# Masks of one head pair moved from TensorE to GpSimd, with task priorities and lags from a timing model, in a windowed-attention and MLP-mixer kernel

## The chip, the cores and the metric

The kernel runs on one core of one Trainium2 chip. Times are device microseconds (us) of one execution. A core has five engines that work in parallel, each taking its own instructions strictly in order: TensorE (PE in the profile; PEld are its weight loads), VectorE (DVE), ScalarE (ACT), GpSimd (POOL), and SyncE (SP), which here issues transfers (DMA). An instruction waits until the data it needs have been announced by a semaphore, and everything behind it in the same engine's queue waits too (in the first timeline below ScalarE stands 2.83 us in front of one instruction). SBUF is the memory of the core in which the engines find their operands; PSUM banks (`ps_ga`, `ps_sb` and so on) are the buffers into which TensorE writes its results, and in this program another engine empties a bank before TensorE uses it again.

## The reference, cut to what matters

Four batches, 8 heads, 768 positions, head size 64. Each position sees the 4 first positions (the sinks) and the last 128. The attention result `x` goes through a token mixer and a channel mixer.

```python
scores = scale * np.matmul(q, k.transpose(0, 1, 3, 2))
keep = is_sink | ((rel >= 0) & (rel < window))        # window = 128, 4 sinks
a = softmax(np.where(keep, scores, -1e9))
x = np.matmul(a, v)                                   # then (B, S, H*D)
u = x + (relu(x.T @ w_tok1) @ w_tok2).T               # token mixer
out = u + relu(u @ w_ch1) @ w_ch2                     # channel mixer
```

## The kernel before

Work is cut into *groups* of 4 heads, two groups per batch, eight in all; a group has two *head pairs*, `j` = 0 and 1. So pair (1,0) is the first pair of the second group of the first batch. The program is a list of tasks, each with dependencies, a priority and an assumed duration. Before anything is emitted, `Plan.order` plays them through a timing model of the engines, and the order found there is the order in which each engine gets its instructions. Nothing is reordered on the chip.

The parts that matter, with cuts marked `# ...`:

```python
PE_MASKS = {0, 1}                      # groups whose masks TensorE adds
DMA_LAG, LATE_LAG, LATE_AT = 1.0, 4.0, 85
BIAS = {}                              # priority offsets by task
LATE_CAST = [None, None, ("POOL", "ACT", "DVE"), ("POOL", "ACT", "DVE"), ("POOL", "ACT", "DVE")]
MASK_ENG = {g: ("POOL",) if g > 3 else ("POOL", "DVE") for g in range(8)}
# ... in the model: when the model believes that a load has landed
finish(x.pop(0)[0], drained + (LATE_LAG if drained > LATE_AT else DMA_LAG if drained > 14 else 1.0))
# ... scores of one unit; with a TensorE mask, -30000 is put into the bank first
if first:
    for i in range(2):
        nc.tensor.matmul(bank(slot)[:, i, 0:w], ident, mneg[...], start=True, stop=False)
for kt, w in kts_of(u)[0]:
    for i in range(2):
        nc.tensor.matmul(bank(slot)[:, i, at:at + w], kT[...], qT[...], start=not first, ...)
# ... exp by ScalarE into pT; without a TensorE mask, pT is then multiplied or
#     selected to zero outside the window, by GpSimd or VectorE (m0, m1)
# ... group 4's loads of q and k are held back until the load of v of group 3 has landed
nc.sync.dma_start(out=scratch_b[0:1, 1:2], in_=va[(g - 1) % 2][...])
# ... each load of q or k (float32) is cast to bfloat16 by one engine out of LATE_CAST[g]
copy(t, dst[s][:, ts(j, NT)], src[s][:, 2 * j:2 * j + 2])
```

The softmax here doesn't subtract the row's maximum and nothing guards it: scores larger than these inputs give would overflow.

Of the kernel before, what the change touches and what calls it, by code (L numbers as in the profile page):

```python
# [14 lines left out]

LOADS = "v0 v1 tok1 tok2 ch1a ch1b ch1c ch2a ch2b q2 k2 v2 q3 k3 v3".split()
CAST_LOADS = set()
PE_MASKS = {0, 1}
DMA_TURNS = {5, 6, 7}
NO_GATE = True  # L20
EARLY, EARLY_PRIO = 4, 1.7
GATE_AT = (1, 1)
GATED = True
FIRST_CASTS = [["ACT", "DVE"], [("POOL", "DVE")] * 2, [("POOL", "DVE")] * 2, [("POOL", "DVE")] * 2]
V_PARTS = 1
DMA_CAST_PARTS = 2
DMA_LAG, LATE_LAG, LATE_AT = 1.0, 4.0, 85
BIAS = {}
ACT_MORE = 0.0
LATE_CAST = [None, None, ("POOL", "ACT", "DVE"), ("POOL", "ACT", "DVE"), ("POOL", "ACT", "DVE")]  # L30
MASK_ENG = {g: ("POOL",) if g > 3 else ("POOL", "DVE") for g in range(8)}

SEM = 0.05
PE_TAIL = 0.16


class Task:


    def __init__(self, eng, hold, fn, deps=(), prio=50, lat=None, need=None, slot=None, frees=False, dma=None, port=False):  # L40
        self.eng = (eng,) if isinstance(eng, str) else tuple(eng)
        self.hold, self.fn, self.prio = hold, fn, prio
        self.lat, self.need, self.slot, self.frees, self.dma = lat, need, slot, frees, dma
        self.port = port
        self.deps = [d for d in deps if d is not None]
        self.start = self.done = None
        self.left, self.users = 0, []

# [8 lines left out]
class Plan:  # L57
# [16 lines left out]
    def order(self, filler=None):  # L74
        for n, t in enumerate(self.tasks):
            t.n = n
            t.left = len(t.deps)
            for d in t.deps:
                d.users.append(t)
# [132 lines left out]
def pe(*cols):  # L212
    return sum(c / 2400 + 0.0025 for c in cols)
# [10 lines left out]
def pool(n, per=0.00086, base=0.12):  # L224
    return n * per + base
# [7 lines left out]
def kernel(  # L233
# [140 lines left out]
    def rows_in_turn(src, g, lo, hi):  # L374
        return heads(src, g, lo, hi).rearrange("h (p t) d -> p h (t d)", t=NT)
# [17 lines left out]
    def pair32(tile_, s, lo, hi):  # L393
        return tile_[s][:, lo:hi].rearrange("p h t d -> p h (t d)")
# [2 lines left out]

    def load_pair(g, which, j, eng, deps=(), prio=5):
        src, dst = ((q, q32), (k, k32))[which]
        return load(eng, pair32(dst, Gs[g].s, 2 * j, 2 * j + 2), rows_in_turn(src, g, 2 * j, 2 * j + 2), 1.12, deps, prio)  # L400

    for g in range(GB):
        for j in range(2):
            if g in CAST_LOADS:
                continue
            Gs[g].lq[j] = load_pair(g, 0, j, "SP", prio=next(order_prio))
            Gs[g].lk[j] = load_pair(g, 1, j, "ACT", prio=0)

    def load_v(g, deps=(), prio=5):
        n = GH // V_PARTS  # L410
# [11 lines left out]
    c1, c2 = DCH // N1, NF // N2  # L422
    L = {}
    for n, what in enumerate(LOADS):
        prio = EARLY_PRIO + 0.001 * n if n < EARLY else 3 + n
        gate = [gate_task] if n >= EARLY and GATED else []
        kind, g = what[:-1], what[-1]
        if kind == "v":
            L[what] = load_v(int(g), gate, prio=prio)
        elif kind in ("q", "k"):  # L430
            g = int(g)
            src, big, small = (q, q32, qb) if kind == "q" else (k, k32, kb)
            if g in CAST_LOADS:
                dst = small[g % 2].rearrange("p a i d -> p (a i d)").rearrange("p (h x) -> p h x", h=GH)
            else:
                dst = pair32(big, g % 2, 0, GH)
            L[what] = load("POOL", dst, rows_in_turn(src, g, 0, GH), 2.6 if g in CAST_LOADS else 2.1, gate if g else [], prio=prio)
        elif what == "tok1":
            L[what] = load("POOL", w_tok1, moe_w_tok1.rearrange("(t p) n -> p t n", p=P), 2.8, gate, prio=prio)
        elif what == "tok2":  # L440
            L[what] = load("POOL", w_tok2, moe_w_tok2.rearrange("(t p) n -> p t n", p=P), 2.2, gate, prio=prio)
        elif kind == "ch1":
            i = ts("abc".index(g), c1)
            L[what] = load("POOL", w_ch1[:, :, i], moe_w_ch1.rearrange("(t p) n -> p t n", p=P)[:, :, i], 2.85, gate, prio=prio)
        elif kind == "ch2":
            i = ts("ab".index(g), c2)
            L[what] = load("POOL", w_ch2[:, i], moe_w_ch2.rearrange("(t p) n -> p t n", p=P)[:, i], 4.3, gate, prio=prio)
# [50 lines left out]
    def pr(g, what, j=0):  # L498
        like = KIND.get(what, what)
        extra = BIAS.get(f"{what}{g}", 0) + (BIAS.get(f"{what}{g}.{j}", 0) if j else 0)  # L500
        if what == "ex" and g not in PE_MASKS:
            extra += 20
        if g < GB:
            return FIRST[like] + 0.5 * g + extra
        return (g // GB) * 10 + CH[like] + 0.5 * (g % GB) + extra
# [46 lines left out]
    def make_cast(g, w, j):  # L552
        G, s = Gs[g], g % 2
        old = Gs[g - 2] if g >= 2 else None
        src, dst, ld = ((q32, qb, G.lq), (k32, kb, G.lk))[w]
        free = [t for t in old.T[w]] if old else []
        if G.dma:
            n = GH // DMA_CAST_PARTS
            G.cast[w] = []
            for j in range(DMA_CAST_PARTS):  # L560
                def f(t, j=j):
                    copy(t, dst[s].rearrange("p a i d -> p (a i d)").rearrange("p (t h d) -> p h t d", t=NT, h=GH)[:, n * j:n * j + n],
                         src[s][:, n * j:n * j + n])
                G.cast[w].append(add("POOL", pool(384 * n), f, [*ld[n * j:n * j + n], *free], prio=pr(g, "ca")))
        elif g in CAST_LOADS:
            G.cast[w] = list(ld)
        else:
            def f(t):
                copy(t, dst[s][:, ts(j, NT)].rearrange("p t i d -> p i t d"), src[s][:, 2 * j:2 * j + 2])
            if g < GB:  # L570
                eng, hold = FIRST_CASTS[2 * g + j][w], {"POOL": pool(768), "DVE": 0.42, "ACT": act(768, True)}
            elif not G.dma:
                eng, hold = LATE_CAST[g], {"POOL": pool(768), "ACT": act(768, True), "DVE": 0.42}
            else:
                eng, hold = ("POOL",), pool(768)
            t = G.cast[w][j] = add(eng, hold, f, [ld[j], *free], prio=pr(g, "ca", j), port=True)
            if (g, j) == GATE_AT and w:
                gate_task.deps.append(t)

    def make_cv(g):  # L580
        G, s = Gs[g], g % 2

        G.cv = list(G.lv)
        if g < 2:
            G.cv.append(add("POOL", 0.12, lambda t: nc.gpsimd.memset(va[s][:, :, :, D:D1], 1.0), prio=1))

    def qkT(T, g, j):
        x = T[g % 2]
# [4 lines left out]
    def make_turn(g, w):  # L593
# [9 lines left out]
            G.T[w] = [t, t]  # L603
            return
        for j in range(2):
            slot = Slot()

            def f(t, j=j, slot=slot):
                ps = flat(slot).bitcast(BF16)
                for n in range(NT):  # L610
                    if g in CAST_LOADS:
                        x = (qb, kb)[w][s].rearrange("p a i d -> p (a i d)").rearrange("p (h t d) -> p h t d", h=GH, d=D)
                        for i in range(2):
                            nc.tensor.transpose(ps[ds(64 * i, 64), ts(n, P)], x[:, 2 * j + i, n], ident)
                        continue
                    else:
                        x = (qb, kb)[w][s][:, j * NT + n].rearrange("p i d -> p (i d)")
                    nc.tensor.transpose(ps[:, ts(n, P)], x, ident)

            m = add("PE", pe(*[P] * NT), f, [G.cast[w][j], t_ident], prio=pr(g, "tr", j), need=("g", 1), slot=slot)  # L620

            def e(t, j=j, slot=slot):
                ps = flat(slot).bitcast(BF16)[:, 0:NT * P].rearrange("d (t p) -> d p t", t=NT)
                copy(t, T[s][:, ts(j, NT)].rearrange("d t p -> d (t p)").rearrange("d (p t) -> d p t", t=NT), ps)

            G.T[w][j] = add(("ACT", "DVE"), either(NT * P), e, [m, *free], prio=pr(g, "tc", j), slot=slot, frees=True)

    def make_ks(g):
        G, s = Gs[g], g % 2
# [16 lines left out]

    def make_scores(g):
        G, s = Gs[g], g % 2
        first = g in PE_MASKS
        units = [(j, u) for j in range(2) for u in range(3)]  # L650
        G.burst = []
        G.exp = {}
        G.ready = {}
        oldpv = Gs[g - 2].pv if g >= 2 else []
        size = 1 if first else 2
        for n in range(0, 6, size):
            todo = units[n:n + size]
            slots = [Slot() for _ in todo]

            def f(t, todo=todo, slots=slots):  # L660
                if first:
                    for (j, u), slot in zip(todo, slots):
                        w = kts_of(u)[1]
# [28 lines left out]
                G.exp[j, u] = add("ACT", act(2 * w), e, [m, *oldpv], prio=pr(g, "ex", j), slot=slot, frees=True)  # L692
        for j in range(2):
            dst = pT[2 * s + j]
            if first:
                for u in range(3):
                    G.ready[j, u] = [G.exp[j, u]]
                continue
# [355 lines left out]
```

## Time and profile before

| | before |
|---|---|
| median of 6 runs (range) | 208.76 us (208.47 to 208.88) |
| span of the profiled run | 207.4 us (this execution took 209.36 us, more than any of the 6 runs) |
| TensorE busy, share of the span | 197.9 us, 95% |
| ScalarE, VectorE, GpSimd busy | 54%, 44%, 35% |
| longest waits of TensorE after 6 us | 2.03, 0.82, 0.59 us |

These lines are from the profile's page of the kernel before: its first part (busy time, share of the span, number of instructions) and its second part, in which the span is cut into 40 slices of 5.2 us and a digit is the busy share of one slice in tenths.

```profile
PE 197.9 (95%) x1622; PEld 115.6 (56%) x1639; DVE 91.6 (44%) x218; ACT 111.5 (54%) x189; POOL 73.5 (35%) x126
...
PE   7889999999978999999999999999999999999993
...
DMA  5999999999689949997995999900012532001122
```

TensorE is full except at the start, at the end and in the 12th and 13th slices (57 to 67 us). The DMA engines are full from 5 to 52 us: the loads for all the early work are one long queue.

The next lines are TensorE's waits in the kernel before: who waited for whom, us in total, times, longest.

```profile
PE ps_ga L765 <- ACT qTa L321: 2.0, 1, 2.0
...
PE ps_sa L672 <- ACT kTa L321: 0.8, 1, 0.8
PE ps_ga L618 <- DVE qbb L323: 0.6, 1, 0.6
```

The first one is the hole at 61 to 63 us: a matmul of group 2 needs PSUM bank `ps_ga`, which ScalarE must first empty by copying `qTa` out. Why ScalarE was late stands in its own timeline (start, duration, then engine, line, operation, output and input; in brackets the idle time before it and what ended it):

```profile
57.03 0.62 ACT L321 ACTIVATE oa<-ps_ga 128x512 f32<-128x512 f32 x1
60.48 0.84 ACT L321 ACTIVATE kba<-k32a 128x768 bf16<-128x768 f32 x1 [2.83 <-DMA k32a<-in_k_dram]
61.23 1.01 ACT L690 ACTIVATE pTc<-ps_sa 128x1024 bf16<-128x1024 f32 x1
62.13 0.80 ACT L321 ACTIVATE qTa<-ps_ga 128x768 bf16<-128x768 bf16 x1
```

ScalarE stood 2.83 us in front of one cast whose load (`k32a`, k of group 4) had not landed. The `qTa` copy, which frees TensorE's bank, was behind it in the queue. The load itself was issued by SyncE late, as soon as the load of v of group 3 (`vab`) had landed, which the `scratch_b` transfer waits for:

```profile
51.68 0.71 SPq L518 DMA_DIRECT2D scratch_b<-vab  x1
52.57 0.91 SPq L366 DMA_DIRECT2D q32a<-in_q_dram  x2
53.58 0.92 SPq L366 DMA_DIRECT2D k32a<-in_k_dram  x2
```

### The profile page before, as it was taken

What the parts mean: (1) busy time and instruction counts of PE and PEld (TensorE: products, weight loads), DVE (VectorE), ACT (ScalarE), POOL (GpSimd) and SP (SyncE); (2) the same over time, 40 slices, a digit from 0 to 9 for tenths busy, and PEclk for the clock granted to TensorE, in tenths of its full rate; (3) what the DMA queues carried; (4) which work ended last, traced back from release to release, by engine and by line L of the source; (5) the groups of instructions that cost most, each with busy time, mean ns of one, the idle gap of its engine ahead of it and who ended that gap; (6) DMA issues with size and microseconds to landing.
All of it is one profiled execution on the core that took longest, in us unless ns stands there. A gap on an engine that the chain in (4) does not pass through costs nothing.

```text
span 207.4 us, 4185 instructions
## 1 busy us (share of the span) xinstructions
PE 197.9 (95%) x1622; PEld 115.6 (56%) x1639; DVE 91.6 (44%) x218; ACT 111.5 (54%) x189; POOL 73.5 (35%) x126
## 2 busy tenths in 40 slices
PE   7889999999978999999999999999999999999993
PEld 2434776666556564667555544557574445655453
DVE  7678650158759866825701123348157122001122
ACT  2798568798849764764363300987620303753200
POOL 8919630011116299993310141689800000000000
PEclk9999999999999999999999999999999999999999
DMA  5999999999689949997995999900012532001122
GB/s 181 364 195 188 207 207 231 309 306 105 195 224 254 145 116 142 155 171 174 178 129 112 235 248 243 187 0 5 0 54 44 133 126 101 3 0 51 51 104 101
DMA packets 74869, 30.97 MB, mean 149 GB/s; under 512 B 63650, under 2 KB 71202, under 8 KB 74850
## 3 DMA queue, kind: packets, MB, share of 16 engines
q0 software_dynamic: 29680, 10.22, 42.2%
q1 hardware_dynamic: 43938, 18.85, 42.0%
q10 hardware_dynamic: 1232, 1.64, 2.2%
q8 instruction: 13, 0.21, 0.4%
q14 instruction: 6, 0.05, 0.1%
HBM read 26.77 MB, written 6.29 MB: 159 GB/s over the span
## 4 chain that ended last, share of the span: by engine, by line
PE 82%; DMA 10%; ACT 2%; DVE 2%; issue 1%; POOL 0%; SPq 0%; POOLq 0%; DVEq 0%; ACTq 0%
PE ps_gb L933 8%; PE ps_ga L914 8%; PE ps_gc L933 8%; PE ps_gc L914 7%; PE ps_gb L914 7%; PE ps_gd L914 7%; PE ps_ga L933 7%; DMA vaa<-in_v_dram 6%; PE ps_gd L933 5%; DMA k32a<-in_k_dram 3%; PE ps_sa L672 3%; PE ps_sb L672 2%; PE ps_ga L836 1%; PE ps_gc L836 1%; PE ps_gb L836 1%; PE ps_gd L878 1%
## 5 line engine op out<-in xcount | busy, mean ns | idle before, releaser
L914 PEld LDWEIGHTS <-w_ch 128*128 128x128 bf16 x384 | 36.7, 98 | 25.8 <-issue 0.8
L933 PEld LDWEIGHTS <-v 128*128 128x128 bf16 x312 | 28.7, 98 | 28.2 <-issue 0.9
L933 PE MATMUL ps_gb<-w_ch,v 128*128 128x512 bf16 (+1 forms) x90 | 22.7, 365 | 0.4 <-issue 0.2
L933 PE MATMUL ps_gc<-w_ch,v 128*128 128x512 bf16 (+1 forms) x82 | 19.5, 356 | 0.1
L933 PE MATMUL ps_ga<-w_ch,v 128*128 128x512 bf16 (+1 forms) x79 | 19.1, 355 | 0.4 <-issue 0.2
L895 ACT ACTIVATE v<-ps_ga 128x384 bf16<-128x384 f32 x24 | 11.8, 490 | 13.4 <-PE ps_ga L914 8.6
L895 ACT ACTIVATE v<-ps_gb 128x384 bf16<-128x384 f32 x18 | 8.8, 490 | 14.4 <-PE ps_gb L914 14.2
L895 ACT ACTIVATE v<-ps_gc 128x384 bf16<-128x384 f32 x18 | 8.8, 490 | 10.6 <-PE ps_gc L914 10.4
L895 ACT ACTIVATE v<-ps_gd 128x384 bf16<-128x384 f32 x21 | 10.3, 492 | 7.3 <-PE ps_gd L914 6.9
L323 POOL CAST kba<-k32a 128x768 bf16<-128x768 f32 x4 | 3.3, 826 | 29.3 <-DMA k32a<-in_k_dram 29.3
L933 PE MATMUL ps_gd<-w_ch,v 128*128 128x512 bf16 x48 | 12.3, 379 | 0.0
L914 PE MATMUL ps_ga<-uTb,w_ch 128*128 128x384 bf16 x56 | 11.4, 326 | 0.0
L948 DVE TENSOR_TENSOR oc<-ps_gb,u_sbb 128x512 f32<-128x512 f32 x2 | 1.4, 692 | 22.5 <-PE ps_gb L933 13.6
L836 PEld LDWEIGHTS <-w_tok 128*128 128x128 bf16 x96 | 9.2, 98 | 2.0 <-issue 0.4
L914 PE MATMUL ps_gb<-uTa,w_ch 128*128 128x384 bf16 x48 | 9.8, 326 | 0.0
L914 PE MATMUL ps_gc<-uTa,w_ch 128*128 128x384 bf16 x48 | 9.8, 326 | 0.0
L914 PE MATMUL ps_gb<-uTb,w_ch 128*128 128x384 bf16 x48 | 9.8, 326 | 0.0
L914 PE MATMUL ps_ga<-uTa,w_ch 128*128 128x384 bf16 x48 | 9.8, 326 | 0.0
L914 PE MATMUL ps_gd<-uTa,w_ch 128*128 128x384 bf16 x48 | 9.8, 326 | 0.0
L690 ACT ACTIVATE pTa<-ps_sa 128x1024 bf16<-128x1024 f32 (+1 forms) x8 | 7.3, 918 | 4.3 <-PE ps_sa L672 4.3
L690 ACT ACTIVATE pTc<-ps_sa 128x1024 bf16<-128x1024 f32 (+1 forms) x8 | 7.3, 914 | 4.0 <-PE ps_sa L672 4.0
L914 PE MATMUL ps_gc<-uTb,w_ch 128*128 128x384 bf16 x44 | 9.0, 326 | 0.0
(328 smaller groups left out, 433.6 us busy)
## 6 DMA issues: line engine op xcount, KB each, us to landing
q32a<-in_q_dram SPq DMA_DIRECT2D x4, 384.0 KB, 3.6
vaa<-in_v_dram POOLq DMA_DIRECT2D x4, 384.0 KB, 11.2
vab<-in_v_dram POOLq DMA_DIRECT2D x4, 384.0 KB, 10.3
w_ch<-in_moe_w_ch_dram POOLq DMA_DIRECT2D x3, 512.0 KB, 9.5
w_ch<-in_moe_w_ch_dram POOLq DMA_DIRECT2D x2, 768.0 KB, 16.1
q32b<-in_q_dram SPq DMA_DIRECT2D x8, 192.0 KB, 3.7
out_dram<-oa SPq DMA_DIRECT2D x6, 256.0 KB, 2.0
k32b<-in_k_dram SPq DMA_DIRECT2D x8, 192.0 KB, 4.3
```

What stands on the lines that cost most here:

```text
L323: on(t).tensor_copy(out=o, in_=i)
L672: nc.tensor.matmul(bank(slot)[:, i, at:at + w].rearrange("p (c q) -> p c q", q=P), qkT(kT, g, j)[ds(64 * i, 64), kt], qkT(qT, g, j)[ds(64 ...
L690: nc.scalar.activation(dst[:, :, 512 * u:512 * u + w], bank(slot)[:, :, 0:w], AF.Exp, scale=scale)
L836: nc.tensor.matmul(flat(slot)[:, 0:GH * D], w_tok1[:, n, ts(tt, P)], x[:, n, ds(a * GH * D, GH * D)], start=(n == 0), stop=(n == NT - 1))
L878: nc.tensor.matmul(flat(slot), w_tok2[:, tt, ts(st, P)], h[:, tt], start=(tt == 0), stop=(tt == NTOK - 1))
L895: nc.scalar.activation(o, i, AF.Relu)
L914: nc.tensor.matmul(flat(slot)[:, 0:HS], w_ch1[:, c, ts(ft, P)], uT_[:, c, ds(half * HS, HS)], start=(c == 0), stop=(c == NC - 1))
L933: nc.tensor.matmul(flat(slot)[:, 0:cw], v1[:, ft, ts(st, P)], w_ch2[:, ft, ds(c0, cw)], start=(ft == 0), stop=(ft == NF - 1 and b > 0), sk ...
L948: nc.vector.tensor_tensor(out=o[:, 0:cw], in0=flat(slot)[:, 0:cw], in1=u[:, st, ds(c0, cw)], op=ALU.add)
```

## The change

Intent: take six mask matmuls (pair (1,0)) away from TensorE, the fullest engine, and let GpSimd mask that pair after the exp; choose mask and cast engines by group; make the model's landing times of loads longer; and offset 34 priorities so that the model's schedule is better. The rest of the diff is plumbing that is switched off (`HALVES` is empty, `K_QUEUE` is as before): with the old constants put back, the changed file builds the same instructions in the same order as the kernel before. Its core:

```diff
-PE_MASKS = {0, 1}
+PE_MASKS = {(0, 1), (1, 1), (0, 0)}
-DMA_LAG, LATE_LAG, LATE_AT = 1.0, 4.0, 85
-BIAS = {}
+DMA_LAG = 1.2
+LATE_LAG = 4.0
+LATE_AT = 57
+BIAS = {'ca2': 15, 'ut3': -0.6, 'tok11': -0.3, 'ca2.1': -8, 'ex7': -4, 'pv4': -15, ... }    # cut: 34 entries
-LATE_CAST = [None, None, ("POOL", "ACT", "DVE"), ("POOL", "ACT", "DVE"), ("POOL", "ACT", "DVE")]
-MASK_ENG = {g: ("POOL",) if g > 3 else ("POOL", "DVE") for g in range(8)}
+LATE_CAST = [None, None, ('POOL', 'ACT', 'DVE'), ('POOL',), ('POOL', 'ACT', 'DVE')]
+MASK_ENG = {0: ('POOL',), 1: ('POOL',), 2: ('DVE',), 3: ('POOL', 'DVE'), 4: ('POOL',), 5: ('POOL',), 6: ('POOL', 'DVE'), 7: ('POOL',)}
 # ... cut: load_pair, make_cast and make_turn can work in halves (not used)
-        if what == "ex" and g not in PE_MASKS:
+        if what == "ex" and g >= GB:
             extra += 20
-        first = g in PE_MASKS
-        size = 1 if first else 2
+        size = 1 if g < GB else 2
         for n in range(0, 6, size):
+            first = (g, todo[0][0]) in PE_MASKS
-            if first:
+            if (g, j) in PE_MASKS:
                 for u in range(3):
                     G.ready[j, u] = [G.exp[j, u]]
                 continue
```

More of the change, by code (lines that the diff above doesn't have):

```diff
@@ L17, with flat_list @@
 CAST_LOADS = set()
-PE_MASKS = {0, 1}
+PE_MASKS = {(0, 1), (1, 1), (0, 0)}
 DMA_TURNS = {5, 6, 7}
 NO_GATE = True
-EARLY, EARLY_PRIO = 4, 1.7
+EARLY = 4
+EARLY_PRIO = 1.7
 GATE_AT = (1, 1)
 GATED = True
-FIRST_CASTS = [["ACT", "DVE"], [("POOL", "DVE")] * 2, [("POOL", "DVE")] * 2, [("POOL", "DVE")] * 2]
+FIRST_CASTS = [['ACT', 'DVE'], [('POOL', 'DVE'), ('POOL', 'DVE')], [('POOL', 'DVE'), ('POOL', 'DVE')], [('POOL', 'DVE'), ('POOL', 'DVE')]]
 V_PARTS = 1
 DMA_CAST_PARTS = 2
-DMA_LAG, LATE_LAG, LATE_AT = 1.0, 4.0, 85
-BIAS = {}
-ACT_MORE = 0.0
-LATE_CAST = [None, None, ("POOL", "ACT", "DVE"), ("POOL", "ACT", "DVE"), ("POOL", "ACT", "DVE")]
-MASK_ENG = {g: ("POOL",) if g > 3 else ("POOL", "DVE") for g in range(8)}
+DMA_LAG = 1.2
+LATE_LAG = 4.0
+LATE_AT = 57
+BIAS = {'ca2': 15, 'ut3': -0.6, 'tok11': -0.3, 'ca2.1': -8, 'ex7': -4, 'pv4': -15, 'lv4': 0.6, 'tc3': -1.6, 'sc3': 2, 'ut2': -8, 'ex3':
+    -8, 'ex4.1': 8, 'ks1': 1, 'mk4.1': -2, 'ca3': -2, 'tr1.1': -2, 'tc3.1': -4, 'sc0.1': -1, 'sc3.1': -1, 'sk3': -0.3, 'tc1.1': -0.6,
+    'mk0.1': 15, 'pv3': 4, 'ut0': 8, 'ex2': -0.3, 'sk2': -1, 'mk0': -15, 'ks2': 4, 'ex4': 0.3, 'sink': 0.6, 'lv0': -4, 'ca3.1': 1,
+    'sc7': -0.6, 'tc4.1': 8}
+ACT_MORE = 0
+LATE_CAST = [None, None, ('POOL', 'ACT', 'DVE'), ('POOL',), ('POOL', 'ACT', 'DVE')]
+MASK_ENG = {0: ('POOL',), 1: ('POOL',), 2: ('DVE',), 3: ('POOL', 'DVE'), 4: ('POOL',), 5: ('POOL',), 6: ('POOL', 'DVE'), 7: ('POOL',)}
+HALVES = set()
+K_QUEUE = ['ACT', 'ACT', 'ACT', 'ACT']
 SEM = 0.05
 PE_TAIL = 0.16
+def flat_list(x):
+    return [z for y in x for z in (flat_list(y) if isinstance(y, (list, tuple)) else [y])]
 class Task:
@@ L44, in __init__ @@
         self.port = port
-        self.deps = [d for d in deps if d is not None]
+        self.deps = list(deps)
         self.start = self.done = None
@@ L76, in order @@
             t.n = n
+            t.deps = [d for d in flat_list(t.deps) if d is not None]
             t.left = len(t.deps)
@@ L399, in load_pair @@
         src, dst = ((q, q32), (k, k32))[which]
-        return load(eng, pair32(dst, Gs[g].s, 2 * j, 2 * j + 2), rows_in_turn(src, g, 2 * j, 2 * j + 2), 1.12, deps, prio)
+        n = 2 if (g, j) in HALVES else 1
+        w = NT * D // n
+        return [load(eng, pair32(dst, Gs[g].s, 2 * j, 2 * j + 2)[:, :, ts(x, w)], rows_in_turn(src, g, 2 * j, 2 * j + 2)[:, :, ts(x, w)],
+                     1.12 / n, deps, prio + 0.001 * x) for x in range(n)]
     for g in range(GB):
@@ L406 @@
             Gs[g].lq[j] = load_pair(g, 0, j, "SP", prio=next(order_prio))
-            Gs[g].lk[j] = load_pair(g, 1, j, "ACT", prio=0)
+            Gs[g].lk[j] = load_pair(g, 1, j, K_QUEUE[2 * g + j], prio=0.01 * (2 * g + j) if K_QUEUE[2 * g + j] == "ACT" else next(order_prio))
     def load_v(g, deps=(), prio=5):
@@ L424 @@
     for n, what in enumerate(LOADS):
-        prio = EARLY_PRIO + 0.001 * n if n < EARLY else 3 + n
+        prio = (EARLY_PRIO + 0.001 * n if n < EARLY else 3 + n) + BIAS.get("L" + what, 0)
         gate = [gate_task] if n >= EARLY and GATED else []
@@ L567, in make_cast, with f @@
         else:
-            def f(t):
-                copy(t, dst[s][:, ts(j, NT)].rearrange("p t i d -> p i t d"), src[s][:, 2 * j:2 * j + 2])
+            n = 2 if (g, j) in HALVES else 1
+            m = NT // n
             if g < GB:
-                eng, hold = FIRST_CASTS[2 * g + j][w], {"POOL": pool(768), "DVE": 0.42, "ACT": act(768, True)}
-            elif not G.dma:
+                eng, hold = FIRST_CASTS[2 * g + j][w], {"POOL": pool(768 // n), "DVE": 0.065 + 0.355 / n, "ACT": act(768 // n, True)}
+            else:
                 eng, hold = LATE_CAST[g], {"POOL": pool(768), "ACT": act(768, True), "DVE": 0.42}
-            else:
-                eng, hold = ("POOL",), pool(768)
-            t = G.cast[w][j] = add(eng, hold, f, [ld[j], *free], prio=pr(g, "ca", j), port=True)
+            t = []
+            for x in range(n):
+                def f(t, x=x):
+                    copy(t, dst[s][:, ts(j, NT)][:, m * x:m * x + m].rearrange("p t i d -> p i t d"), src[s][:, 2 * j:2 * j + 2, m * x:m * x + m])
+                t.append(add(eng, hold, f, [ld[j][x] if n > 1 else ld[j], *free], prio=pr(g, "ca", j), port=True))
+            G.cast[w][j] = t
             if (g, j) == GATE_AT and w:
@@ L584, in make_cv @@
         if g < 2:
-            G.cv.append(add("POOL", 0.12, lambda t: nc.gpsimd.memset(va[s][:, :, :, D:D1], 1.0), prio=1))
+            G.cv.append(add("POOL", 0.12, lambda t: nc.gpsimd.memset(va[s][:, :, :, D:D1], 1.0), prio=0.1))
     def qkT(T, g, j):
@@ L605, in make_turn @@
         for j in range(2):
-            slot = Slot()
-            def f(t, j=j, slot=slot):
-                ps = flat(slot).bitcast(BF16)
-                for n in range(NT):
-                    if g in CAST_LOADS:
-                        x = (qb, kb)[w][s].rearrange("p a i d -> p (a i d)").rearrange("p (h t d) -> p h t d", h=GH, d=D)
-                        for i in range(2):
-                            nc.tensor.transpose(ps[ds(64 * i, 64), ts(n, P)], x[:, 2 * j + i, n], ident)
-                        continue
-                    else:
-                        x = (qb, kb)[w][s][:, j * NT + n].rearrange("p i d -> p (i d)")
-                    nc.tensor.transpose(ps[:, ts(n, P)], x, ident)
@@ L620, in make_turn @@
-            m = add("PE", pe(*[P] * NT), f, [G.cast[w][j], t_ident], prio=pr(g, "tr", j), need=("g", 1), slot=slot)
-            def e(t, j=j, slot=slot):
-                ps = flat(slot).bitcast(BF16)[:, 0:NT * P].rearrange("d (t p) -> d p t", t=NT)
-                copy(t, T[s][:, ts(j, NT)].rearrange("d t p -> d (t p)").rearrange("d (p t) -> d p t", t=NT), ps)
-            G.T[w][j] = add(("ACT", "DVE"), either(NT * P), e, [m, *free], prio=pr(g, "tc", j), slot=slot, frees=True)
+            parts = 2 if (g, j) in HALVES else 1
@@ new lines, in make_turn, with f, e @@
+            m_ = NT // parts
+            G.T[w][j] = []
+            for x in range(parts):
+                slot = Slot()
+                def f(t, j=j, slot=slot, x=x, m_=m_, parts=parts):
+                    ps = flat(slot).bitcast(BF16)
+                    for n in range(m_ * x, m_ * x + m_):
+                        if g in CAST_LOADS:
+                            y = (qb, kb)[w][s].rearrange("p a i d -> p (a i d)").rearrange("p (h t d) -> p h t d", h=GH, d=D)
+                            for i in range(2):
+                                nc.tensor.transpose(ps[ds(64 * i, 64), ts(n, P)], y[:, 2 * j + i, n], ident)
+                            continue
+                        y = (qb, kb)[w][s][:, j * NT + n].rearrange("p i d -> p (i d)")
+                        nc.tensor.transpose(ps[:, ts(n, P)], y, ident)
+                c = G.cast[w][j]
+                m = add("PE", pe(*[P] * m_), f, [c[x] if parts > 1 else c, t_ident], prio=pr(g, "tr", j), need=("g", 1), slot=slot)
+                def e(t, j=j, slot=slot, x=x, m_=m_):
+                    ps = flat(slot).bitcast(BF16)[:, ds(m_ * x * P, m_ * P)].rearrange("d (t p) -> d p t", t=m_)
+                    copy(t, T[s][:, ts(j, NT)].rearrange("d t p -> d (t p)").rearrange("d (p t) -> d p t", t=NT)[:, :, m_ * x:m_ * x + m_], ps)
+                G.T[w][j].append(add(("ACT", "DVE"), either(m_ * P), e, [m, *free], prio=pr(g, "tc", j), slot=slot, frees=True))
@@ L658, in make_scores, with f @@
             slots = [Slot() for _ in todo]
-            def f(t, todo=todo, slots=slots):
+            first = (g, todo[0][0]) in PE_MASKS
+            def f(t, todo=todo, slots=slots, first=first):
                 if first:
```

## The prediction

> **What bounds it now.** TensorE: by the page's first part 95% busy (197.9 of 207.4 us); the chain of waits is 82% TensorE; clock fully granted. In TensorE's timeline the first real matmul starts at 6.03 us, the last ends at about 204; outside that the change does nothing. All matmuls between, costed at their observed spacing (two 512-column masks 0.43 us, four 384-column channel matmuls 0.65, a 65-column one 0.031), take an estimated 193.1 us. The Trainium skill ("TensorE: Matmul & The Clock Gate", Back-to-back issue gap) has about 216 ns for 512 columns; the trace agrees. So about 4.9 us can be won by ordering. The view of waits: 2.03 us at 60.95 us (sink matmul of group 2), 0.82 at 7.6, 0.59 at 11.1, some of 0.16, and about 0.1 us at each of 12 switches from mask matmuls (128 rows) to score matmuls (64 rows).
>
> **Removed.** Six mask matmuls of pair (1,0): 0.43+0.43+0.33 = 1.2 us, 1.5 with the switches. (By the diff it is the first pair of the second head group.)
>
> **Added.** GpSimd masks that pair after the exp: in the timeline at 72 to 78 us the same work on another pair takes 1.12+1.44+1.7 = 4.2 us. The skill ("GPSIMD Engine Reference", Engine selection) says about twice DVE's time for two inputs; this trace has 1.15 against 0.41 us. It falls at 17 to 23 us, where GpSimd issues loads (w_ch from 16.4, q and k of group 2 from 20.3), and delays some by up to 4 us; harmless if the DMA engines (90% busy there) have queued work and w_ch lands before 31.7 us.
>
> **On the critical path.**
> 1. Early stage: ScalarE is nearly full from 8.9 to 23.2 us (twelve exps of about 0.9 us, copies; idle 0.8). So TensorE's 1.2 to 1.5 us shorten it by only about 0.8, partly by tok1 of group 0 moving up.
> 2. The 2.03 us stall: TensorE waits for a bank that ScalarE must empty (qTa copy, 62.13). ScalarE stood 2.83 us before the cast of k of group 4, whose load, issued at 53.58, landed at 60.4; the old plan allows 1 us after transfer until 85 us, the new one 4 us from 57 us on, and group 2's masks go to DVE, group 3's casts to GpSimd. I expect the stall mostly gone (1.5 us).
> 3. Priorities: some of the 0.82+0.59 and small pieces, 0.4 us.
> 4. Against it: new waits where the model errs (GpSimd masks late for group 1's PV; group 3's casts on GpSimd alone at 0.83 us each), 0.4 us.
>
> From 100 us on TensorE is full; nothing to gain. 0.8+1.5+0.4-0.4 = 2.3 us: 208.8 becomes 206.4 us, range 204.4 to 208.4. More than 2% (below 204.6) needs nearly all of the 4.9 us.
>
> **What would show it.** Mask matmuls 18 instead of 24, TensorE busy about 1.5 us less; first channel matmul at about 30.9 instead of 31.7 us; no wait over 0.5 us for ScalarE's qTa copy at 58 to 64 us; no ScalarE idleness before group 4's k cast; GpSimd selects on pTc between 16 and 24 us; ScalarE still nearly full to 23 us; 100 us to the end as long as before.
>
> **What would make it wrong.** The in-order queues: a task put early on a load that lands late stops its engine, and the stall only moves (then about 208). GpSimd masks delaying group 1's PV by over 1 us, or holding w_ch back. Or the new order removes nearly all waits: 204.4.
>
> Chances: faster by over 2% 0.13, within 2% 0.83, slower by over 2% 0.04.

## The result, and the profile after

The changed kernel takes 207.19 us (median of 6 runs, 206.78 to 207.90), against 208.76 us (208.47 to 208.88) before. A ratio in this document is in essence the mean time of one kernel's runs over that of the other's runs of the same rounds, so it is not quite the ratio of the medians quoted. Here it is 0.9932, with a 95% interval of 0.9911 to 0.9954: faster by 0.7%, which is within 2%. The runs of the changed kernel scatter over 1.1 us, those of the kernel before over 0.4 us.

The page's lines of the kernel after that answer to those shown above:

```profile
PE 198.4 (97%) x1633; PEld 115.4 (56%) x1633; DVE 97.1 (47%) x230; ACT 109.5 (53%) x184; POOL 72.9 (35%) x123
...
PE   7889999999989999999999999999999999999993
...
DMA  5999999999499959999969968620012442001122
```

TensorE's busy time did not fall, although it has six matmuls fewer (1633 weight loads, one per matmul, against 1639). The busy time before came from 1622 matmul records for 1639 matmuls; 17 records were missing from that trace, none here. Busy time of TensorE is therefore not the number to judge by. TensorE's waits in the kernel after:

```profile
PE ps_gb L789 <- DVE x_bb L816: 0.9, 1, 0.9
PE ps_sa L696 <- ACT kTa L334: 0.7, 1, 0.7
PE ps_ga L640 <- DVE qbb L336: 0.6, 1, 0.6
PE ps_gd L794 <- DMA vaa<-in_v_dram: 0.3, 1, 0.3
```

The 2.03 us wait for ScalarE is gone; a wait of 0.86 us for VectorE stands at the same place. The two early waits are there as before. VectorE's timeline in the kernel after shows the cause of the 0.86 us:

```profile
57.19 0.42 DVE L816 TENSOR_TENSOR x_bb<-ps_gc,rcb 128x256 bf16<-128x256 f32 x1
58.80 0.56 DVE L336 CAST qba<-q32a 128x768 bf16<-128x768 f32 x1 [1.19 <-DMA q32a<-in_q_dram]
59.89 0.56 DVE L336 CAST kba<-k32a 128x768 bf16<-128x768 f32 x1 [0.53 <-DMA k32a<-in_k_dram]
60.36 0.17 DVE L815 RECIPROCAL rcc<-ps_gb 128x4 f32<-128x4 f32 x1
60.57 0.42 DVE L816 TENSOR_TENSOR x_bb<-ps_gb,rcc 128x256 bf16<-128x256 f32 x1
```

It is the same fault on another engine. VectorE stands 1.19 and 0.53 us in front of two casts of group 4, and the normalisation that frees bank `ps_gb` is behind them. SyncE issued those loads half a microsecond later than before:

```profile
52.26 0.70 SPq L534 DMA_DIRECT2D scratch_b<-vab  x1
53.08 0.91 SPq L379 DMA_DIRECT2D q32a<-in_q_dram  x2
54.09 0.42 SPq L379 DMA_DIRECT2D k32a<-in_k_dram  x1
```

### A ledger of TensorE's time

To see where 1.8 us of the span went (207.4 to 205.6), I made an account. The medians are only 1.57 us apart: the profiled execution of the kernel before was 0.6 us longer than its median, that of the changed kernel 0.1 us. The account takes the program's own list of matmuls, in order, and matches it to the trace, so that missing records do no harm. Each matmul is charged its columns at the full rate plus 2.5 ns. The Trainium skill ("TensorE: Matmul & The Clock Gate", Back-to-back issue gap) gives this as the gap of an isolated matmul, and other figures for streams (see the last section). These traces agree with the isolated figure: four matmuls of 384 columns take 0.65 us, four of 512 take 0.86 to 0.87 us. Score matmuls on 64 rows are charged three quarters of their columns, which is how the trace spaces them (four in 0.32 to 0.33 us). The sum of the charges is *work*; the time in which TensorE did less than that is *lost*. It is an estimate, good to about 0.2 us. "Lost to 52 us" includes about 3.7 us before the first real matmul starts.

| profiled run | work | first channel matmul | lost to 52 us | lost 52–70 us | lost after 70 us | last matmul group starts |
|---|---|---|---|---|---|---|
| before | 193.47 | 31.72 | 7.54 | 2.44 | 0.57 | 203.80 |
| after | 192.28 | 30.54 | 7.52 | 1.81 | 0.58 | 201.97 |

So 1.19 us of the difference is work taken away, about 0.63 us is the shorter stall between 52 and 70 us, and nothing else changed in sum. By this table the two gains simply add. The experiments show that they don't. (The 0.63 us is about as large as the excess of that one execution of the kernel before. The better comparison comes below: drop10 has the changed kernel's amount of work in the order of the kernel before, and lost 2.57 us between 52 and 70 us where the changed kernel lost 1.81.)

### The profile page after: what moved, and what is told of

It is laid out like the page before. It is cut to its first block, busy times and chain, and to the rows that moved or that the text cites. A ratio compares the mean times of both kernels' runs of the same rounds, so it can differ in the third digit from the quotient of the medians.

```text
span 205.6 us, 4197 instructions
## 1 busy us (share of the span) xinstructions
PE 198.4 (97%) x1633; PEld 115.4 (56%) x1633; DVE 97.1 (47%) x230; ACT 109.5 (53%) x184; POOL 72.9 (35%) x123
## 4 chain that ended last, share of the span: by engine, by line
PE 85%; DMA 9%; DVE 3%; issue 1%; POOL 0%; SPq 0%; POOLq 0%; DVEq 0%
PE ps_gd L938 9%; PE ps_ga L957 8%; PE ps_gb L938 8%; PE ps_ga L938 8%; PE ps_gb L957 7%; DMA vaa<-in_v_dram 7%; PE ps_gc L957 7%; PE ps_gd L957 6%; PE ps_gc L938 6%; DMA k32a<-in_k_dram 3%; PE ps_sb L696 3%; PE ps_sa L696 2%; PE ps_gc L860 2%; PE ps_ga L860 1%; PE ps_gb L860 1%; DVE pTa L734 1%
## 5 line engine op out<-in xcount | busy, mean ns | idle before, releaser
L957 PE MATMUL ps_ga<-w_ch,v 128*128 128x512 bf16 (+1 forms) x96 | 23.4, 366 | 0.0
L957 PE MATMUL ps_gd<-w_ch,v 128*128 128x512 bf16 x72 | 18.5, 379 | 0.0
L957 PE MATMUL ps_gb<-w_ch,v 128*128 128x512 bf16 (+1 forms) x72 | 16.6, 352 | 0.0
L957 PE MATMUL ps_gc<-w_ch,v 128*128 128x512 bf16 (+1 forms) x72 | 16.4, 352 | 0.0
L725 POOL TENSOR_TENSOR pTc<-pTc,mask 128x512 bf16<-128x512 bf16 x3 | 3.5, 1151 | 23.1 <-ACT pTc L714 23.1
L336 POOL CAST kbb<-k32b 128x768 bf16<-128x768 f32 x6 | 5.4, 920 | 17.2 <-DMA k32b<-in_k_dram 17.2
L938 PE MATMUL ps_gd<-uTb,w_ch 128*128 128x384 bf16 x56 | 11.4, 326 | 0.0
L379 POOL DMA_DIRECT2D vaa<-in_v_dram x4 | 6.0, 1493 | 12.0 <-PE ps_gc L798 11.1
L714 ACT ACTIVATE pTa<-ps_sb 128x1024 bf16<-128x1024 f32 (+1 forms) x7 | 6.5, 929 | 6.2 <-PE ps_sb L696 6.2
L336 POOL CAST qbb<-q32b 128x768 bf16<-128x768 f32 x7 | 6.1, 884 | 6.3 <-DMA q32b<-in_q_dram 6.3
```

The source lines that it names most:

```text
L336: on(t).tensor_copy(out=o, in_=i)
L379: t = add(eng, hold, lambda t: e.dma_start(out=o, in_=i), deps, prio=prio, dma=work)
L714: nc.scalar.activation(dst[:, :, 512 * u:512 * u + w], bank(slot)[:, :, 0:w], AF.Exp, scale=scale)
L725: on(t).tensor_tensor(out=dst[:, :, 0:2 * P], in0=dst[:, :, 0:2 * P], in1=mask0.rearrange("p i c q -> p i (c q)"), op=ALU.mult)
L938: nc.tensor.matmul(flat(slot)[:, 0:HS], w_ch1[:, c, ts(ft, P)], uT_[:, c, ds(half * HS, HS)], start=(c == 0), stop=(c == NC - 1))
L957: nc.tensor.matmul(flat(slot)[:, 0:cw], v1[:, ft, ts(st, P)], w_ch2[:, ft, ds(c0, cw)], start=(ft == 0), stop=(ft == NF - 1 and b > 0), sk ...
```

## The experiments

The theory: (A) The time is set where an engine stands, in its fixed order, before a cast of group 4 whose load lands at about 59 to 60.5 us, a time that TensorE's progress does not move. Work taken from TensorE before that point only makes it wait longer there. The mask move pays only as far as that stall is also removed.

The rivals: (B) TensorE's work simply adds up, and the stall is a fixed cost of 2 us; (C) the priorities are what gained; (D) the early stage is bound by ScalarE, or GpSimd's masks cost something there.

All experiments in one table first; the kernel before was run again in each of the three rounds of experiments, with medians of 208.82, 208.93 and 208.69 us. In each of these rounds one of its eleven runs lies about 2 us above the median (211.01, 210.77, 210.91 us, granted clock 0.99), and one of drop10's four lies 1.6 us above its own (210.36 us, 0.99); they are in the ratios, and the medians are hardly moved by them.

| run | median (range), us | ratio to before (95%) |
|---|---|---|
| mask_only | 208.63 (207.57 to 209.66) | 0.9982 (0.9940 to 1.0024) |
| no_bias | 207.81 (206.82 to 208.82) | 0.9941 (0.9901 to 0.9981) |
| cast4_pool | 206.49 (206.16 to 206.92) | 0.9877 (0.9841 to 0.9913) |
| before_cast4_pool | 207.40 (207.19 to 207.85) | 0.9926 (0.9893 to 0.9960) |
| mask_cast4 | 207.73 (207.03 to 208.14) | 0.9934 (0.9900 to 0.9967) |
| double10 | 208.41 (208.28 to 209.54) | 0.9982 (0.9942 to 1.0023) |
| drop10 (wrong result) | 208.76 (208.64 to 210.36) | 1.0013 (0.9962 to 1.0063) |
| lag_only | 209.79 (208.13 to 210.66) | 1.0021 (0.9978 to 1.0064) |
| bc4_drop10 (wrong result) | 206.70 (206.56 to 206.82) | 0.9893 (0.9854 to 0.9932) |
| late50 | 206.78 (206.25 to 207.52) | 0.9895 (0.9857 to 0.9933) |
| late50_c4 | 208.06 (207.40 to 208.44) | 0.9954 (0.9919 to 0.9988) |
| nopool10 (wrong result) | 207.25 (206.91 to 207.53) | 0.9919 (0.9879 to 0.9958) |

### mask_only: the mask move alone

```diff
 # the changed kernel, with the old constants back except PE_MASKS
-BIAS = {...}   -DMA_LAG = 1.2   -LATE_AT = 57   # and the new LATE_CAST, MASK_ENG
+BIAS = {}      +DMA_LAG = 1.0   +LATE_AT = 85   # old LATE_CAST and MASK_ENG, group 1 on POOL
```

> The change's mask move alone: pair (1,0) on GpSimd, all priorities, lags, cast and mask engines as before. Theory A (TensorE's work is the bound in the early stage): TensorE loses 1.19 us of work (6 masks) and the first channel matmul starts about 1.2 us earlier than the kernel before's 31.7 us; the stall near 61 us stays about 2 us, because the plan still counts on k of group 4 at about 57.9 us, now in front of VectorE; total about 207.6. Theory B (ScalarE or the GpSimd masks bound the early stage): first channel matmul within 0.5 us of 31.7 us, total over 208.3.

Measured: 208.63 us median, six runs between 207.57 and 209.66; not distinguishable from the kernel before. In the profiled run (207.90 us, one of the quicker) the first channel matmul starts at 30.33 us, 1.4 us earlier, so the early stage did gain what TensorE lost in work. By 52 us this kernel is ahead, and then it loses 2.07 us between 52 and 70 us. TensorE now waits 1.33 us for VectorE, which stood 1.11 us in front of a cast of q of group 4. Here the matmul that waits is the transposition of that very q: what stood too early was TensorE's own work on the late load, not another task behind the cast. The part of A about the early stage held; its total of 207.6 missed by 1 us. The gain of the mask move is there at 30 us and gone at the end.

### no_bias: the whole change without the priorities

```diff
-BIAS = {'ca2': 15, 'ut3': -0.6, ...}
+BIAS = {}
```

> The whole change without its 38 priority offsets. Theory A (the offsets give nothing: the two waits of 0.7 and 0.6 us at 8 and 11 us and the small gaps are the same in both traces): within 0.3 us of the changed kernel's 207.2. Rival (the offsets are what gained): 208 or more.

Measured: 207.81 us, 0.6 us slower than the changed kernel, with runs from 206.82 to 208.82. Neither number was met, and the two ratios' intervals (0.9901 to 0.9981 and 0.9911 to 0.9954) overlap. In its profile the waits of 0.8 and 0.6 us at 8 and 11 us are as everywhere, and the wait for VectorE that ends at 61.8 us is 1.69 us instead of 0.86. What the priorities give is therefore not resolved: 0.6 us by the medians, 0.2 us by the ratios, which were taken in different rounds. In the profiled runs the difference is seen at the same stall. C as the main cause falls: most of the gain is there without the priorities.

### cast4_pool and before_cast4_pool: nobody but GpSimd stands before the late loads

```diff
 # in the changed kernel, and in the kernel before:
-LATE_CAST = [None, None, ..., ..., ('POOL', 'ACT', 'DVE')]
+LATE_CAST = [None, None, ..., ..., ('POOL',)]
```

> The kernel before with only the casts of group 4 moved to GpSimd. Theory A (its 2.03 us stall is ScalarE standing 2.83 us before a cast whose load lands late): stall below 0.5 us, total about 206.8 to 207.3. Rival (TensorE is short of other work until k of group 4 has landed): the stall stays or moves, over 208.2.

> The changed kernel with all four casts of group 4 on GpSimd, which has nothing else to do there. Theory A (TensorE's 0.86 us at 61 us comes from VectorE standing 1.19+0.53 us before casts whose loads have not landed, ahead of the normalisations that free the banks): that wait is below 0.2 us, total 206.3 to 206.6, less spread than the changed kernel's 206.8 to 207.9. Rival (VectorE simply has too much to do there, or TensorE waits for the loads themselves): no gain, 207.2, and the wait stays or comes back a few us later.

Measured: the kernel before with this one edit takes 207.40 us, 1.4 us less and as good as the whole change (0.9926 against 0.9932). The stall at 61 us is gone altogether. GpSimd does the waiting (the two casts of k in GpSimd's timeline of before_cast4_pool), and nothing that TensorE needs soon is behind it:

```profile
60.31 0.83 POOL L323 CAST kba<-k32a 128x768 bf16<-128x768 f32 x1 [2.03 <-DMA k32a<-in_k_dram]
61.47 0.83 POOL L323 CAST kba<-k32a 128x768 bf16<-128x768 f32 x1 [0.33 <-PE ps_sa L672]
```

The `qTa` copy, which had been behind the cast on ScalarE (62.13 us), is now VectorE's and is done before k lands:

```profile
60.11 0.95 DVE L323 COPY qTa<-ps_ga 128x768 bf16<-128x768 bf16 x1
```

This shows the mechanism: the load landed no earlier (60.3 us), TensorE had other work, and what had held it up was the queue behind the cast. The edit is not quite alone, though, because the model plans anew from it: besides the casts and this copy, a group of 15 matmuls of TensorE went behind two groups of scores, and a few instructions of ScalarE and VectorE changed place or engine; all else kept its order.

The changed kernel with the same edit takes 206.49 us, faster by the medians than both kernels of the change (all six of its runs are at 206.92 us or below; four of the changed kernel's six are above that). It was as expected in total and in spread (0.8 us), but one part missed: a wait of 0.65 us for VectorE stayed. VectorE no longer waits for a load there; two mask pieces took 1.77 us while GpSimd was casting, as VectorE's timeline of cast4_pool shows, next to the same operation in the changed kernel, four pieces in 1.46 us:

```profile
59.82 1.77 DVE L734 TENSOR_TENSOR pTd<-pTd,mask 128x512 bf16<-128x512 bf16 x2
```

```profile
55.36 1.46 DVE L734 TENSOR_TENSOR pTb<-pTb,mask 128x512 bf16<-128x512 bf16 x4
```

The Trainium skill says that GpSimd shares its SBUF interfaces with VectorE and that VectorE instructions with two SBUF inputs contend ("GPSIMD Engine Reference", Specifications). The masks here are such instructions, and the slow ones overlap GpSimd's work, so the traces agree; that sharing is the cause of the slowness was not tested by itself. A count over all 14 traces points the same way: 267 mask multiplies of this size on VectorE had no computing GpSimd instruction beside them and took 0.41 to 0.49 us each, and every longer one, up to 1.81 us, was overlapped by GpSimd's work.

### double10 and drop10: more and less work for TensorE, order untouched

```diff
 # the kernel before; double10: the six mask matmuls of pair (1,0) twice, result unchanged
-for i in range(2):
+for i in (0, 1, 0, 1) if (g, j) == (1, 0) else (0, 1):
 # drop10: left out, wrong result on purpose
-def f(t, todo=todo, slots=slots):
+def f(t, todo=todo, slots=slots, first=first and not (g == 1 and todo[0][0] == 0)):
```

> The kernel before, its order untouched, with the six mask matmuls of pair (1,0) issued twice (the second overwrites the first, the result stays right): TensorE has 1.2 us more work before 24 us. Theory A (the stall near 61 us ends at a time that loads set, issued at 51.7 us when an earlier load has landed, not when TensorE is done): first channel matmul 1.2 us later (32.9), the stall shrinks from 2.03 to about 0.8 us, total unchanged, 208.6 to 209.1. Rival (all of TensorE's work adds up): stall still 2.0 us, total 210.0.

> The kernel before, its order untouched, with the six mask matmuls of pair (1,0) left out and nothing in their place (wrong result on purpose). Theory A (load-set end of the stall): first channel matmul at about 30.5 us, stall about 3.2 us, total about 208.5, so the work taken away is given back. Rival (TensorE's work adds up): stall 2.0 us, total 207.6.

Measured: with 1.19 us of work more, 208.41 us; with 1.19 us less, 208.76 us; the kernel before beside them 208.93 us. Neither is distinguishable from it. B would have had 210 and 207.6 us. TensorE's waits, first of double10, then of drop10 (their first channel matmuls start at 33.08 and 30.66 us, 2.4 us apart, as the edit says; the lines with `warm` and `qba` are the start-up, before 6.2 us):

```profile
PE ps_ga L1014 <- DVE warm L327: 1.3, 1, 1.3
PE ps_sa L672 <- ACT kTa L321: 0.7, 1, 0.7
PE ps_gd L770 <- DMA vaa<-in_v_dram: 0.6, 1, 0.6
PE ps_ga L618 <- DVE qbb L323: 0.6, 1, 0.6
PE ps_ga L618 <- ACT qba L321: 0.4, 1, 0.4
```

```profile
PE ps_gc L765 <- DVE x_bb L792: 1.2, 1, 1.2
...
PE ps_ga L765 <- ACT qTa L321: 0.5, 1, 0.5
```

In double10 no wait at 61 us is left at all; in drop10 there are two, 1.20 and 0.49 us. Lost time between 52 and 70 us:

| profiled run | work | lost 52–70 us | sum |
|---|---|---|---|
| double10 | 194.66 | 0.24 | 194.90 |
| before | 193.47 | 2.44 | 195.91 |
| drop10 | 192.28 | 2.57 | 194.85 |

Work and lost time go opposite ways from drop10 to double10 and their sum is the same within 0.1 us. The profiled run of the kernel before stands 1 us above both, and its trace gives a reason: the same load took longer. The line is of each load's time from issue to landing, for `k32a` between 50 and 66 us in the kernel before:

```profile
DMA to landing us min/median/max: 6.8/6.8/6.8
```

In double10 it was 5.4 us, in drop10 5.6 us, in the changed kernel 5.7 us. So the expected stall lengths (0.8 and 3.2 us) missed while the landing itself varied by more than 1 us between these three executions; that this variation is why they missed is the likely reading, not a tested one. The totals, over several runs, came out as A expected.

That TensorE's progress doesn't move the landing is seen in the `scratch_b` line that starts these loads: 51.75 us in double10, 52.00 in drop10, 51.68 before, 52.26 after, while TensorE's first channel matmul ranges from 30.54 to 33.08 us. What it waits for is the load of v of group 3. GpSimd issues that between 29.96 us (double10) and 30.32 us (drop10), and it takes over 21 us to land, because the DMA engines are full up to 52 us.

### lag_only: only the model's lags

```diff
 # the kernel before
-DMA_LAG, LATE_LAG, LATE_AT = 1.0, 4.0, 85
+DMA_LAG, LATE_LAG, LATE_AT = 1.2, 4.0, 57
```

> The kernel before with only the two lags of the timing model changed (1.2 us, and 4 us from 57 us on). Its plan still puts the first cast of q and of k of group 4 on ScalarE and VectorE at 56.1, 57.0 and 58.0 us, and only the second k cast later (64.1). Theory A (casts placed before their loads have landed are the stall): k lands at about 60, so a stall of 1 to 2 us stays, total 207.8 to 208.8. Rival (the lags alone remove the stall): 207.2 or less.

Measured: 209.79 us median, from 208.13 to 210.66: no gain, perhaps a loss (ratio 1.0021, not distinguishable from 1). My upper figure of 208.8 was too low. Between 52 and 70 us the profiled run loses 1.75 us, 0.7 us less than before, but a new wait of 0.87 us appears at 131.9 us. Longer lags from 57 us on come too late for loads that the model lets land at 57 to 58 us, and a new order has its own accidents.

### mask_cast4 and bc4_drop10: is the mask move worth its 1.2 us once the stall is gone?

```diff
 # mask_cast4: mask_only, and
-LATE_CAST[4]: ('POOL', 'ACT', 'DVE')
+LATE_CAST[4]: ('POOL',)
 # bc4_drop10: before_cast4_pool, and (wrong result on purpose, order untouched)
-def f(t, todo=todo, slots=slots):
+def f(t, todo=todo, slots=slots, first=first and not (g == 1 and todo[0][0] == 0)):
```

> The mask move alone (as in mask_only) together with the casts of group 4 on GpSimd; everything else as in the kernel before. Theory A (the mask move's 1.2 us is real but mask_only lost it to the engine that stands before the late loads): gains add, 1.4 us (before_cast4_pool) plus 1.2 us, total 206.1 to 206.4, as fast as cast4_pool or faster, with none of the priorities or lags. Rival (the mask move is worth nothing on its own, as mask_only's median says): 207.4, like before_cast4_pool.

> before_cast4_pool, its order untouched, with the six mask matmuls of pair (1,0) left out and nothing in their place (wrong result on purpose): drop10's edit where the stall near 61 us is gone. Theory A (what keeps TensorE's saving from showing is only the engine that stands before the late loads): total 206.2, 1.2 us under before_cast4_pool's 207.4. Rival (a later point is set by loads too, the casts on GpSimd wait for k until 60.3 us all the same): 206.8 to 207.4, with a wait of up to 1.2 us somewhere in 60 to 80 us.

Measured: mask_cast4 takes 207.73 us. The expectation of 206.1 to 206.4 failed, and the rival's 207.4 is the nearer one. The stall at 61 us is gone (0.64 us lost between 52 and 70 us), but 2.18 us are lost after 70 us, against 0.54 in before_cast4_pool: the mask move changed the plan's choices later on. VectorE masks pair (3,1) while GpSimd first casts k of group 5 and then masks pair (4,0), and both are slow: four mask pieces in 3.00 us on VectorE (1.46 us in the line above), the 512-element multiply in 1.43 us on GpSimd (1.15 us elsewhere). These are VectorE's and GpSimd's lines of mask_cast4:

```profile
68.68 3.00 DVE L731 TENSOR_TENSOR pTd<-pTd,mask 128x512 bf16<-128x512 bf16 x4
```

```profile
69.97 1.43 POOL L722 TENSOR_TENSOR pTa<-pTa,mask 128x512 bf16<-128x512 bf16 x1 [0.20 <-ACT pTa L711]
```

TensorE waits 0.35 and 0.62 us for that. bc4_drop10, which keeps the order, takes 206.70 us: 0.7 us under before_cast4_pool, where A said 1.2 and the rival 0 to 0.6, so that the number is nearer the rival's. The work is 1.19 us less, and the trace shows about half a microsecond given back between 52 and 70 us (0.95 us lost there, against 0.47), of which 0.42 us is a wait for a mask of pair (3,1) on VectorE. The intervals of the two ratios overlap (0.9854 to 0.9932 and 0.9893 to 0.9960), the single runs do not; they were made on different chips. So with the stall gone TensorE's saving begins to show, but not all of it: the next limit is close behind.

### late50 and late50_c4: tell the model when the loads land

```diff
 # the changed kernel; late50_c4 also has LATE_CAST[4] = ('POOL',)
-LATE_AT = 57
+LATE_AT = 50
```

> The changed kernel with the 4 us lag counted from 50 us on instead of 57: its plan then has the loads of group 4 landing at 60 to 61 us, as measured, and puts no cast of them before 61.7 us on VectorE. Theory A (the wrong landing time in the model is what left 0.86 us of wait in the changed kernel): no wait over 0.3 us at 58 to 64 us, total about 206.4, spread below 1 us. Rival (any order has some such wait): 207.2.

> Both remedies: the 4 us lag from 50 us on, and the casts of group 4 on GpSimd only. Theory A: as late50 or 0.2 us better, 206.0 to 206.4. Rival (GpSimd's casts and VectorE's masks get in each other's way, as in cast4_pool where two mask pieces took 1.77 us instead of 0.75): as cast4_pool, 206.5, or slower.

Measured: late50 takes 206.78 us. No wait is left between 58 and 64 us (0.60 us lost between 52 and 70 us, against 1.81), as A said; VectorE casts q of group 4 at 61.49 us without idling. The total is 0.4 us above what A said, and the spread is 1.3 us and not under 1: 1.67 us are lost after 70 us, 0.6 us of that in a wait at 94.75 us for a transposing transfer of k. So a second remedy removes the stall too, by placing the casts of group 4 later (it is a new plan, with TensorE's order changed in many places, and so weaker evidence than before_cast4_pool), and part of the gain is given back at another load. Both remedies together, late50_c4, take 208.06 us: worse than either, with a wait of 1.00 us for VectorE's copy of `qTa` at 68.3 us. The rival was nearer, and the loss was larger than it said. I did not take that apart; the trace does show that two mask pieces on VectorE took 2.14 us just before that copy (65.26 to 67.40 us), while GpSimd was casting (64.22 to 66.79 us), which is what the rival named.

### nopool10: GpSimd's masks of pair (1,0) left out

```diff
 # the changed kernel, order untouched, wrong result on purpose
 def m0(t, dst=dst):
+    if g == 1:
+        return                           # likewise in m1
```

> The changed kernel, its order untouched, without the GpSimd mask instructions of pair (1,0) (wrong result on purpose). Theory A (GpSimd's 4.2 us there cost nothing): first channel matmul within 0.15 us of the changed kernel's 30.5 us, total 207.2 within 0.3. Rival (they delay PV of group 1 or the loads behind them): first channel matmul earlier by 0.4 us or more, or total 206.7 or less.

Measured: 207.25 us, against the changed kernel's 207.19. The first channel matmul starts at 30.19 us instead of 30.54; 0.31 us of that is the changed kernel's wait for `vaa` at 15.6 us, which is before GpSimd's first mask of the pair (17.37 us) and is absent in this run and in late50. So neither number given for the channel matmul was met, for a reason outside the masks. GpSimd's masks cost nothing that can be seen in the total; the last part of D falls. For the first part of D, here are ScalarE's last exp and TensorE's first token-mixer matmul, before and then after:

```profile
22.46 0.81 ACT L690 ACTIVATE pTd<-ps_sb 128x768 bf16<-128x768 f32 x1
```

```profile
24.51 0.82 PE L836 MATMUL ps_gd<-x_ba,w_tok 128*128 128x256 bf16 x6
```

```profile
22.49 0.81 ACT L714 ACTIVATE pTd<-ps_sb 128x768 bf16<-128x768 f32 x1 [0.28 <-PE ps_sb L696]
```

```profile
21.02 0.83 PE L860 MATMUL ps_ga<-x_ba,w_tok 128*128 128x256 bf16 x6
```

The last exp did not move (22.46 and 22.49 us), and TensorE did token-mixer work of group 0 3.5 us earlier than before. From these two traces alone it looks as if ScalarE set the end of the exps. double10 and then drop10, whose order is that of the kernel before, say otherwise. Their last exps:

```profile
23.83 0.81 ACT L690 ACTIVATE pTd<-ps_sb 128x768 bf16<-128x768 f32 x1
```

```profile
21.41 0.81 ACT L690 ACTIVATE pTd<-ps_sb 128x768 bf16<-128x768 f32 x1
```

Counted from TensorE's first matmul that reads v (15.34 us before, 15.51 and 15.46 us here), the last exp starts 7.12 us later before, 8.32 us in double10 and 5.95 us in drop10. That is 1.20 us more and 1.17 us less for 1.19 us of TensorE's work more or less: nearly full as it was, ScalarE followed TensorE. In the changed kernel the exp kept its time because TensorE did token-mixer work (six matmuls in 0.66 us) in front of the scores for it; the line shows ScalarE waiting 0.28 us for them. So the first part of D falls too, and about the same was won by 30 us in drop10 (30.66 us), where nothing was moved up.

## Why the prediction was right or wrong

The total was right: 206.4 us with a range of 204.4 to 208.4, and 207.19 us measured; "within 2%" had the largest chance. The forecast gain of 2.3 us was 1.6 us. Some of that closeness is luck: the early term was too small (0.8 for 1.18 us), the stall's too large (1.5 for about 0.63 us), and the sum that joins them is not sound.

- **"Six mask matmuls ... = 1.2 us, 1.5 with the switches."** 1.19 us of work by the ledger. The switches don't show in the sum: lost time up to 52 us is 7.54 and 7.52 us; but the changed kernel has a 0.31 us wait for `vaa` in that stretch which the kernel before has not, so a gain of about that size may be hidden behind it. As a sign I named TensorE busy 1.5 us less; it rose by 0.5 us, with 17 records missing from the trace before, so that sign was worthless.
- **"So TensorE's 1.2 to 1.5 us shorten it by only about 0.8."** Too small, and for a wrong reason: the first channel matmul moved from 31.72 to 30.54 us, 1.18 us (I had said 30.9). I took a nearly full ScalarE for the limit of the stage. In double10 and drop10 its last exp moved with TensorE's work, by 1.20 and 1.17 us for 1.19 us, so TensorE set the pace. tok1 (the first product of the token mixer) of group 0 did move up, but drop10 won as much without it.
- **"The 2.03 us stall ... I expect the stall mostly gone (1.5 us)."** The mechanism was right, and so was the sign that ScalarE would not be idle before the k cast. The stall became 0.86 us in front of VectorE, which I had named as a danger ("the stall only moves") but not counted. By the ledger it gave 0.63 us in the profiled runs, 0.76 us against drop10. The 2.03 us came from one execution that was 0.6 us longer than the median.
- **"0.8+1.5+0.4-0.4": the step that failed is the addition.** I added the early saving to the shorter stall as if they were independent. double10, drop10 and mask_only show that before the stall a microsecond of TensorE's work is worth nothing as long as the engine in front of the late loads is the limit: 1.19 us more or less left the time where it was. The early saving was paid out because the same change also shortened the stall: drop10, with the saving alone, gained nothing. How much each paid in the change as it stands was not measured. Even with the stall gone, only about 0.7 us of 1.19 came out (bc4_drop10).
- **"Priorities: ... 0.4 us."** The two early waits are still there, 0.70 and 0.59 us (0.82 and 0.59 before). no_bias gives the priorities 0.6 us by the medians and 0.2 us by the ratios, at the stall and not at the early waits; their share is not resolved.
- **"GpSimd masks late for group 1's PV ... 0.4 us" against it.** Nothing: no wait for those masks, and nopool10 is no faster. The time that was given back was at the casts of group 4.
- **The landing time of loads** I took as a fixed fact from one trace. It varies by over 1 us between executions (5.4 to 6.8 us for `k32a`), which is enough to account for spreads of 1 to 2 us in the kernels with an engine standing in front of it; that it is the cause of their spread was not shown.

The best kernel found is the changed one with the casts of group 4 on GpSimd alone: 206.49 us, ratio 0.9877 to the kernel before. Against the changed kernel it was not run in the same rounds; the medians differ by 0.7 us and the ratios' intervals (0.9841 to 0.9913 and 0.9911 to 0.9954) just touch.

Still open: what limits bc4_drop10 and late50_c4 after 60 us, how much of the changed kernel's gain the priorities carry, and how much the mask move does. The whole change without the mask move was not run; the nearest runs give the move nothing (drop10) or about 0.7 us (bc4_drop10), while before_cast4_pool, without it, gains 1.4 us.

## What to carry to other kernels

When each engine works in a fixed order, look for an instruction that waits for a transfer with others' work queued behind it; give such a task to the engine that has nothing urgent behind it, or place it after the measured landing time. A saving on the fullest engine may be given back where a time set by loads lies downstream of it: test that by doubling the work as well as by removing it, with the order kept, before believing a sum of gains. The same test tells whether an engine that looks full is the limit or follows another. A timing model that lands loads too early can put this fault into the orders that it finds, as it did in both kernels here.

## What the Trainium skill lacked or had wrong

- "TensorE: Matmul & The Clock Gate", Back-to-back issue gap, states a sustained spacing of about 131 ns for 512 columns and 81 ns for 128 in streams of weight load and matmul. These traces show 216 ns (four in 0.86 to 0.87 us) and 57 ns (six transposes in 0.34 us), each matmul with its own weight load. They agree with the formula that the page calls the isolated gap.
- "GPSIMD Engine Reference", Engine selection, has GpSimd about twice as slow as VectorE for two inputs. For the 512-element bfloat16 multiply here it is 1.15 us against 0.41 us, 2.8 times.
- "GPSIMD Engine Reference", Specifications, names the contention with VectorE but no size; the skill does treat it at more length on another page, so this is a gap of that section only. Measured here: four mask pieces on VectorE took 1.46 us, and 3.00 us while GpSimd cast and masked; GpSimd's multiply went from 1.15 to 1.43 us.
- No page that I read says how much the landing of the same load varies from run to run: 5.4 to 6.8 us from issue for the same 384 KB load in three kernels with the same order.
